# First queries and keys in halves of partitions, constants made by GpSimd, 28 constant products at the start, first values scaled in two parts

## The chip, the cores and the metric

The kernel runs on one core of one Trainium2 chip. The metric is the device time of one execution in microseconds (us), median of several runs. Four compute engines share the work: TensorE (matrix products; PE in the tables, PEld its weight loads), VectorE (DVE), ScalarE (ACT) and GpSimd (POOL). SyncE (SP) issues most loads and stores; ScalarE's queue issues some.

## The reference, cut to what matters

Retention attention over 8 batches and 8 heads of 576 positions with 64 values each, in fp32, then a mixture of 8 experts over the 4608 resulting rows of 512 values.

```python
scores = scale * np.matmul(q, k.transpose(0, 1, 3, 2))
rel = pos[:, None] - pos[None, :]
Dmat = np.where(rel >= 0, gamma[:, None, None] ** rel[None, :, :], 0.0)
ret = scores * Dmat[None, :, :, :]
return np.matmul(ret, v).astype(np.float32)
...
x = np.ascontiguousarray(attn_out.transpose(0, 2, 1, 3)).reshape(B * S, H * D)
...
expert_idx = np.argmax(logits, axis=1)
gate_w = probs[np.arange(N), expert_idx]
for e in range(E):
    mask = expert_idx == e
    h = np.maximum(x[mask] @ w1[e], 0.0)
    out[mask] = gate_w[mask, None] * (h @ w2[e])
```

## The kernel before

The 4608 rows are taken as 36 tiles of 128 rows, all 8 heads at once; a batch is 4.5 tiles. The first 140 us or so are attention (18 stages of two tiles), with the routing to experts woven in; the rest are the experts one after the other, each product made of three with operands split in a high and a low part.

For tile t, `qkt[t]` holds queries and keys turned (partition = position inside a head; partitions 0 to 63 are one head of each pair and 64 to 127 the other; four pairs), `kvt[t]` keys and values by rows. `emit_A(t)` makes the scores of a tile: for each pair p and half h a product of 64 partitions, to the banks `pa`; then VectorE masks them with the triangle `tri` into `pm`. `turn_k(t)` turns the keys of the first four tiles on TensorE with the identity `ident` (in tile 0 in two halves, to `prow` and `pa[2]`), and ScalarE copies them to `kvt`. `scale_v(t, ...)` scales the values by a power of the decay on GpSimd. `emit_U(t)` adds keys times values to the state (bank `pst`), which ScalarE copies to `T`. `emit_O(t)` multiplies the masked scores with the values to `po`. `decay(k)` makes the factors `gsb` on GpSimd.

The order of the instructions on each engine is that of the code (the schedule is manual); semaphores between engines are set from what each instruction reads and writes. `load_qk` and `load_kv` issue on SyncE; six tiles can be held, and a load of a later tile waits until TensorE has done with the buffer. Tile 0 alone is loaded from two queues: one half of `qkt[0]` by SyncE, followed by the table `cs`, and the other by ScalarE, followed by the values of tile 0.

Before the first scores, TensorE multiplies a constant matrix of bf16 ones with itself `NWARM` times, into `prow` and with no use of the result. In this time VectorE clears some tiles and, as soon as `cs` has landed, makes `tri` and `ident` by comparing the column number `iota` with the partition number `part`, both from `cs`.

Of the kernel before, what the change touches and what calls it, by code (L numbers as in the profile page):

```python
# [15 lines left out]
ALU = mybir.AluOpType  # L16
AX = mybir.AxisListType

P = 128
B, H, S, D = 8, 8, 576, 64  # L20
NP = H // 2
# [17 lines left out]
RW = 1032  # L39
XO = 520  # L40
BIG = 1.0e6
NWARM = 40
NO = NT + 2
HD = P // 2
QD = P // 4
# [6 lines left out]
KT = 9  # L52
# [49 lines left out]
def retention_moe(ctx: ExitStack, tc: tile.TileContext, qk, kv, embT, tau, w1, w2, cst, out):  # L102
    nc = tc.nc
# [26 lines left out]
    def mm(*args, **kw):  # L130
        pe[:] = [nc.tensor.matmul(*args, **kw)]  # L131
        return pe[0]
# [10 lines left out]
    def cc(name):  # L143
        o, w = _C[name]
        return cs[:, o : o + w]
# [24 lines left out]
    ident = keep.tile([P, P], F32, name="ident")  # L170
# [383 lines left out]
    with ExitStack() as att:  # L554
# [11 lines left out]
        qkt, kvt = {}, {}  # L566
# [13 lines left out]
        taub = ap.tile([P, 1], F32, name="taub")  # L580
        qkt[0] = qkp.tile([P, NP, 2, P], F32, name="qkt")
        kvt[0] = qkp.tile([P, 2, H, D], F32, name="kvt")
        nc.sync.dma_start(out=qkt[0][:, : NP // 2], in_=qk[0][:, : NP // 2])
        nc.scalar.dma_start(out=qkt[0][:, NP // 2 :], in_=qk[0][:, NP // 2 :])
        nc.sync.dma_start(out=cs, in_=cst[:, :_FIRST])
        nc.scalar.dma_start(out=kvt[0][:, 1], in_=kv[0][:, 1])
        load_qk(1)
# [14 lines left out]
        warm = psm.tile([P, 512], F32, name="m")  # L602
        for _ in range(NWARM):
            mm(warm[:, :P], one, one, start=True, stop=True)

        tri = ap.tile([P, P], F32, name="tri")
        trix = ap.tile([P, P], F32, name="trix")
        onef = ap.tile([P, P], F32, name="onef")
        iota, part = cc("iota"), cc("part")
        vx = ap.tile([P, H, D], F32, name="vx")  # L610
        E32 = ap.tile([P, NP, EW], F32, name="E32")
        nc.vector.memset(ones, 1.0)
        nc.vector.memset(onef, 1.0)
        nc.vector.memset(half, 0.5)
        nc.vector.memset(tok_all[:, 3 * NT :], 0.0)
        nc.vector.memset(ovs[:, 0:1], 0.0)
        nc.vector.memset(E32, 0.0)
        nc.gpsimd.memset(vx[:D], 0.0)
        nc.vector.tensor_scalar(out=tri, in0=iota, scalar1=part, scalar2=None, op0=ALU.is_ge)
        nc.vector.tensor_scalar(out=ident, in0=iota, scalar1=part, scalar2=None, op0=ALU.is_equal)  # L620

        def constants():
            nc.vector.tensor_copy(trix, tri)
# [25 lines left out]
        def embeddings_scale():  # L649
# [3 lines left out]
            nc.vector.tensor_tensor(  # L653
                out=E32[:, :, :NE], in0=emb, in1=en.unsqueeze(1).broadcast_to([P, NP, NE]), op=ALU.mult
            )
# [5 lines left out]
        gneg = cc("gneg").rearrange("p (t h) -> p t h", t=KT)  # L661
# [12 lines left out]
        def scale_v(t, eng):  # L674
            if t >= NT:
                return
            v = kvt[t][:, 1]
            eng.tensor_tensor(  # L678
                out=v, in0=v, in1=gneg[:, t % KT].unsqueeze(2).broadcast_to([P, H, D]), op=ALU.mult
            )  # L680
            if t % KT == 4:
                eng.tensor_copy(vx[D:], v[D:])

# [111 lines left out]
        def xpair(x, p):  # L795
            return x[..., p & 1, (p >> 1) * P : (p // 2 + 1) * P]
# [21 lines left out]
        def route_logits(b):  # L818
# [4 lines left out]
            for p in range(NP):  # L823
                for g in range(GT):
                    mm(
                        ps[g * EW : (g + 1) * EW, :P],
                        E32[:, p, :],
                        xpair(x[:, g], p),
# [38 lines left out]
        for b in range(NG):  # L867
            s0 = 2 * b + 2
            if s0 < HS:
                at((s0, 1.5), lambda b=b: (on(pa[2]), route_logits(b)))  # L870
                if s0 < LATE:
                    at((s0, 1.8), lambda b=b: (on(pa[2]), route_turn(b, False)))
                    at((s0, 3), lambda b=b: (keep_logits(b), route_head(b)))
                else:
                    at((s0, 3), lambda b=b: (on(pa[2]), route_turn(b), route_head(b)))
                if s0 + 1 < LATE:
                    at((s0 + 1, 1.7), lambda b=b: (on(pa[1]), rank_sum(b)))
                    at((s0 + 1, 2), lambda b=b: rank_slot(b))
                else:
                    at((s0 + 1, 2), lambda b=b: (on(pa[1]), route_rank(b)))  # L880
            if s0 + 2 < HS:
                if s0 + 2 < LATE:
                    at((s0 + 2, 1), lambda b=b: route_onehot(b))
                    at((s0 + 2, 1.7), lambda b=b: (on(pa[1]), route_table(b, False)))
                    at((s0 + 2, 2), lambda b=b: table_add(b))
                else:
                    at((s0 + 2, 3), lambda b=b: route_onehot(b))
                    at((s0 + 3, 2), lambda b=b: (on(pa[2]), route_table(b)))
            if b == EARLY - 1:
                at((s0 + 3, 1.7), lambda: (on(pa[0]), route_bump()))  # L890
                at((s0 + 2, 3), lambda: slots_to_tokens(0, 3))
                at((s0 + 2, 3), lambda t=2 * s0 + 8: scale_v(t, nc.gpsimd))
                for i in range(3):
                    at((s0 + 2, 3), lambda i=i: gather(0, i, EARLY * GT * P))
# [17 lines left out]
        emit_A(0)  # L912
        turn_k(0)
        scale_v(0, nc.gpsimd)
        scale_v(1, nc.gpsimd)
        decay(0)
        decay(1)
# [4 lines left out]
        for s in range(HS):  # L922
            t, u = 2 * s, 2 * s + 1
# [74 lines left out]
    with ExitStack() as moe:  # L998
# [3 lines left out]
        hs = mw.tile([P, 2, NF, CAP], F32R, name="hs")  # L1002
# [403 lines left out]
        for e in range(1, NE):  # L1406
            n = e + 1
# [61 lines left out]
            o = (bank[4], bank[5], bank[6], bank[4], bank[7])  # L1469
# [122 lines left out]
    with tc.If(ntile > 0):  # L1592
        with ExitStack() as ov:
            op = ov.enter_context(tc.tile_pool(name="op", bufs=1))
# [8 lines left out]
                out=io8, in0=cc("iota")[:, :NE], scalar1=float(ES), scalar2=None, op0=ALU.mult  # L1603
# [4 lines left out]
                out=sel, in0=eidx_all.unsqueeze(2).broadcast_to([P, NT, NE]), in1=io8, op=ALU.is_equal  # L1608
            )
            nc.vector.tensor_tensor(  # L1610
                out=sel, in0=sel, in1=ovs[:, :NE].unsqueeze(1).broadcast_to([P, NT, NE]), op=ALU.mult
# [12 lines left out]
                out=tok, in0=entry[:, :, 0], scalar1=float(P), scalar2=cc("part"), op0=ALU.mult, op1=ALU.add  # L1624
            )
            nc.vector.tensor_scalar(out=tok, in0=tok, scalar1=float(1 - P), scalar2=None, op0=ALU.add)
            for t in range(NT):
                nc.gpsimd.indirect_dma_start(
                    out=od[:, :],
                    out_offset=bass.IndirectOffsetOnAxis(ap=dsti[:, t : t + 1], axis=0),  # L1630
                    in_=tok[:, t : t + 1],
# [8 lines left out]
                out=te,  # L1640
                in0=cc("iota")[:, :NO].unsqueeze(2).broadcast_to([P, NO, NE]),
                in1=ovs[:, 1:].unsqueeze(1).broadcast_to([P, NO, NE]),
                op=ALU.is_ge,
# [7 lines left out]
            with tc.For_i(0, ntile, 1) as i:  # L1651
# [9 lines left out]
                    out=of[:, 0:1], in0=ent[:, 0:1], scalar1=-1.0, scalar2=0.0, op0=ALU.add, op1=ALU.max  # L1661
                )
                nc.vector.tensor_scalar(
                    out=of[:, 2:3], in0=ent[:, 0:1], scalar1=0.0, scalar2=BIG, op0=ALU.is_equal, op1=ALU.mult
# [6 lines left out]
                    out=go,  # L1671
                    out_offset=None,
                    in_=gd[:, :],
# [4 lines left out]
                    out=xo,  # L1678
                    out_offset=None,
                    in_=xd[:, :],  # L1680
# [29 lines left out]
                for f in range(NF):  # L1710
# [4 lines left out]
                    out=out[:, :],  # L1715
                    out_offset=bass.IndirectOffsetOnAxis(ap=oi[:, 1:2], axis=0),
                    in_=yo,
# [47 lines left out]
```

## Time and profile before

| | us |
|---|---|
| median of 3 runs | 552.0 (551.15, 552.0, 554.64) |
| profiled execution | 551.2 |
| its span, first to last instruction | 549.3 |
| TensorE busy in the span | 542.1 |
| TensorE's weight loads | 490.9 |
| VectorE | 406.9 |
| ScalarE | 359.0 |
| GpSimd | 213.2 |

The profiled execution is one run; times in its rows are counted from the start of the span. The profiled run's own time is 1.9 us longer than its span.

### The profile page before, as it was taken

How to read it: one execution, taken by the hardware profiler on the slowest of the kernel's cores; microseconds unless marked ns; L12 is line 12 of the kernel's file. 1: busy time of each engine (PE TensorE's matmuls, PEld its weight loads, DVE VectorE, ACT ScalarE, POOL GpSimd, SP SyncE). 2: the span in 40 equal slices, each digit the busy share in tenths (PEclk: the TensorE clock that was granted, in tenths of full speed). 3: DMA queues.
4: the chain of work that ended last, by engine and by line, in shares of the span. 5: the costliest groups of instructions: out<-in, count | busy, mean ns of one | idle time of the engine just before them, and what ended most of it. 6: DMA issues, size and time to landing. Idle time of an engine off the chain costs nothing. (4 is left out here: it accounts for less than half of the span.)

```text
span 549.3 us, 13219 instructions
## 1 busy us (share of the span) xinstructions
PE 542.1 (99%) x5119; PEld 490.9 (89%) x5119; DVE 406.9 (74%) x892; ACT 359.0 (65%) x656; POOL 213.2 (39%) x192
## 2 busy tenths in 40 slices
PE   9999999999999999999999999999999999999996
PEld 8999998889898889889988988998998899889984
DVE  3777789887786877995896899589689848957400
ACT  2455567665846786785786778578777857857311
POOL 4863222337446155067028415702840660161021
PEclk9999999999999999999999999999999999999999
DMA  8999999999567749457836945783692578351001
GB/s 316 384 338 363 392 398 388 371 380 257 193 129 217 195 133 283 76 151 219 185 79 190 277 80 133 228 188 97 178 277 67 152 243 162 94 176 51 4 38 50
DMA packets 83221, 111.70 MB, mean 203 GB/s; under 512 B 48151, under 2 KB 48443, under 8 KB 83136
## 3 DMA queue, kind: packets, MB, share of 16 engines
q1 hardware_dynamic: 75120, 90.00, 55.2%
q0 software_dynamic: 7680, 19.95, 11.0%
q8 instruction: 61, 1.00, 0.7%
q10 hardware_dynamic: 336, 0.54, 0.3%
q14 instruction: 24, 0.20, 0.1%
HBM read 81.10 MB, written 19.94 MB: 184 GB/s over the span
## 5 line engine op out<-in xcount | busy, mean ns | idle before, releaser
L1186 POOL DMA_INDIRECT out<-y,sid x40 | 51.6, 1290 | 157.4 <-ACT y L1182 137.8
L131 PE MATMUL pst<-w2f,hs 128*128 128x512 f32 x360 | 86.6, 390 | 0.0
L131 PE MATMUL po<-w2f,hs 128*128 128x512 f32 x371 | 86.5, 389 | 0.0
L131 PEld LDWEIGHTS po<-w2f,hs 128*128 128x128 f32 x371 | 69.4, 188 | 14.3
L131 PEld LDWEIGHTS pst<-w2f,hs 128*128 128x128 f32 x360 | 66.9, 188 | 13.2
L198 DVE TENSOR_TENSOR w2f<-wraw,w2f 128x1024 fp32r<-128x1024 f32 x32 | 39.1, 1223 | 42.0 <-ACT w2f L194 41.9
L678 POOL TENSOR_TENSOR kvt<-kvt,cs 128x512 f32<-128x512 f32 x36 | 38.3, 1069 | 66.1 <-DMA kvt<-kv 59.0
L442 ACT COPY graw<-graw 128x1024 uint16<-128x1024 uint16 x37 | 50.4, 1363 | 11.5 <-DMA graw<-graw 11.5
L421 POOL DMA_INDIRECT gt<-gd,gid x40 | 46.9, 1173 | 18.4 <-issue 11.6
L131 PE MATMUL prow<-w2f,hs 128*128 128x512 f32 x192 | 46.0, 390 | 0.0
L131 PE MATMUL pa<-xxf,w0f 128*128 128x304 f32 (+3 forms) x312 | 45.5, 297 | 0.0
L695 DVE TENSOR_TENSOR pm<-pa,tri 128x512 f32<-128x512 f32 x64 | 40.0, 682 | 6.9 <-PE pa L131 6.7
L131 PEld LDWEIGHTS pa<-xxf,w0f 128*128 128x128 f32 x312 | 43.0, 188 | 0.1
L131 PEld LDWEIGHTS prow<-w2f,hs 128*128 128x128 f32 x192 | 36.1, 188 | 7.5
L131 PE MATMUL pa<-xsf,w0f 128*128 128x384 f32 (+3 forms) x240 | 38.9, 312 | 0.0
L131 PE MATMUL pa<-qkt 64*128 64x128 f32 x576 | 38.7, 281 | 0.0
L482 DVE TENSOR_TENSOR graw<-graw 128x128 f32<-128x128 f32 x140 | 34.6, 289 | 5.2 <-ACT graw L442 4.0
L492 ACT CAST xxf<-graw 128x128 fp32r<-128x128 f32 x70 | 31.7, 458 | 10.3 <-DVE graw L482 9.9
L194 ACT CAST w2f<-wraw 128x1024 fp32r<-128x1024 f32 x32 | 33.6, 1051 | 6.5 <-DMA wraw<-w 6.4
L131 PEld LDWEIGHTS pa<-qkt 64*128 64x128 f32 x576 | 34.5, 189 | 3.6 <-issue 3.1
L131 PEld LDWEIGHTS pa<-xsf,w0f 128*128 128x128 f32 x240 | 36.2, 188 | 0.3 <-DVE hs L1074 0.3
L131 PE MATMUL po<-pm,kvt 128*64 128x128 f32 (+1 forms) x640 | 35.7, 263 | 0.1
(207 smaller groups left out, 1115.8 us busy)
## 6 DMA issues: line engine op xcount, KB each, us to landing
wraw<-w SPq DMA_DIRECT2D x64, 512.0 KB, 4.4
qkt<-qk SPq DMA_DIRECT2D x35, 512.0 KB, 6.8
kvt<-kv SPq DMA_DIRECT2D x32, 512.0 KB, 8.2
xd<-xw SPq DMA_DIRECT2D x36, 256.0 KB, 4.9
kvt<-kv SPq DMA_DIRECT2D x3, 256.0 KB, 6.6
gt<-gd,gid POOLq DMA_INDIRECT x40, 3.9
out<-y,sid POOLq DMA_INDIRECT x40, 4.0
graw<-xd,gid POOLq DMA_INDIRECT x26, 4.1
```

Of the source, the lines that this page charges most:

```text
L131: pe[:] = [nc.tensor.matmul(*args, **kw)]
L194: nc.scalar.copy(self.to[:, 0, c * 1024 : (c + 1) * 1024], self.raws[c])
L198: nc.vector.tensor_tensor(out=self.to[:, 1, c * 1024 : (c + 1) * 1024], in0=self.raws.pop(c), in1=hi.bitcast(F32), op=ALU.subtract,)
L421: nc.gpsimd.indirect_dma_start(out=g[:, i : i + 1], out_offset=None, in_=gd[:, :], in_offset=bass.IndirectOffsetOnAxis(ap=gid[:, a : a + 1 ...
L442: copy(t[:, :DM].bitcast(U16).rearrange("p (n h) -> p h n", h=2), t[:, XO : XO + DM].bitcast(U16).rearrange("p (h n) -> p h n", h=2),)
L482: nc.vector.tensor_tensor(out=v[:, 2 * k : 2 * k + 2], in0=a, in1=b, op=ALU.subtract)
L492: nc.scalar.copy(x[:, 0], u)
L678: eng.tensor_tensor(out=v, in0=v, in1=gneg[:, t % KT].unsqueeze(2).broadcast_to([P, H, D]), op=ALU.mult)
L695: nc.vector.tensor_tensor(out=pm[:, h], in0=banks[h].rearrange("p (c n) -> p c n", c=NP), in1=m.unsqueeze(1).broadcast_to([P, NP, P]), op= ...
L1186: sc = nc.gpsimd.indirect_dma_start(out=out[:, :], out_offset=bass.IndirectOffsetOnAxis(ap=sid[:, a : a + 1], axis=0), in_=ys[i], in_offse ...
```

## The change

It has four parts, all at the beginning of the program. The two halves of `qkt[0]` are cut by partitions (0 to 63 and 64 to 127, all four pairs each) and no longer by pairs. `ident` and `tri` are made by GpSimd from the matrix of ones `onef`, which VectorE clears first now, with no use of `cs`. `NWARM` is 28 in place of 40. The values of tile 0 are scaled in two products of four heads each; the other tiles as before.

```diff
-NWARM = 40
+NWARM = 28
...
-        nc.sync.dma_start(out=qkt[0][:, : NP // 2], in_=qk[0][:, : NP // 2])
-        nc.scalar.dma_start(out=qkt[0][:, NP // 2 :], in_=qk[0][:, NP // 2 :])
+        nc.sync.dma_start(out=qkt[0][:D], in_=qk[0][:D])
+        nc.scalar.dma_start(out=qkt[0][D:], in_=qk[0][D:])
...
+        nc.vector.memset(onef, 1.0)
+        for to, op in ((ident, ALU.is_equal), (tri, ALU.is_ge)):
+            nc.gpsimd.affine_select(
+                out=to, in_=onef, pattern=[[1, P]], compare_op=op, fill=0.0, base=0, channel_multiplier=-1
+            )
         nc.vector.memset(ones, 1.0)
-        nc.vector.memset(onef, 1.0)
...
         nc.gpsimd.memset(vx[:D], 0.0)
-        nc.vector.tensor_scalar(out=tri, in0=iota, scalar1=part, scalar2=None, op0=ALU.is_ge)
-        nc.vector.tensor_scalar(out=ident, in0=iota, scalar1=part, scalar2=None, op0=ALU.is_equal)
...
-            eng.tensor_tensor(
-                out=v, in0=v, in1=gneg[:, t % KT].unsqueeze(2).broadcast_to([P, H, D]), op=ALU.mult
-            )
+            n = H if t else H // 2
+            for o in range(0, H, n):
+                hs = slice(o, o + n)
+                eng.tensor_tensor(
+                    out=v[:, hs],
+                    in0=v[:, hs],
+                    in1=gneg[:, t % KT, hs].unsqueeze(2).broadcast_to([P, n, D]),
+                    op=ALU.mult,
+                )
```

On GpSimd, from the barrier at the program's start to the scaling of the values of tile 1 (`kvt_137` are the values of tile 0, `kvt_144` those of tile 1; ISA is a set-up instruction of the engine; a bracket names the engines and DMA queues that a row waits for), this stood before:

```order
L1761 UNCONDITIONAL_BRANCH [waits barrier_Pool_Activation_PE_DVE_SP_gather]
L618 MEMSET vx_208 64x512
L678 ISA
L678 TENSOR_TENSOR kvt_137<-kvt_137,cs_83 128x512 [waits DMAHW3_49,DMAHW2_49]
L678 TENSOR_TENSOR kvt_144<-kvt_144,cs_83 128x512 [waits DMAHW5_49]
```

And this stands there now:

```order
L1769 UNCONDITIONAL_BRANCH [waits barrier_Pool_Activation_PE_DVE_SP_gather]
L614 ISA
L614 AFFINE_SELECT ident_101<-onef_195 128x128 [waits DVE_49]
L614 AFFINE_SELECT tri_193<-onef_195 128x128
L622 MEMSET vx_196 64x512
L683 TENSOR_TENSOR kvt_137<-kvt_137,cs_83 128x256 [waits DMAHW3_49,DMAHW2_49]
L683 TENSOR_TENSOR kvt_137<-kvt_137,cs_83 128x256
L683 TENSOR_TENSOR kvt_144<-kvt_144,cs_83 128x512 [waits DMAHW5_49]
```

The two selections and the set-up instruction came in front of the clear of `vx`, and the one product of 512 columns became two of 256.

On TensorE, from the second half of the scores of tile 0 to its state product (`qkt_136` is tile 0; `pa0` and `pa1` are the banks of the two partition halves), before:

```order
L131 MATMUL pa0_73<-qkt_136 128x128 [waits DMAHW0_49]
L131 MATMUL pa1_74<-qkt_136 128x128
L131 MATMUL pa0_73<-qkt_136 128x128
L131 MATMUL pa1_74<-qkt_136 128x128
L135 MATMUL prow_78<-ident_101,qkt_136 128x128 [waits DVE_49]
L135 MATMUL prow_78<-ident_101,qkt_136 128x128
L135 MATMUL pa2_75<-ident_101,qkt_136 128x128 x2
L131 MATMUL pst_77<-kvt_137 64x64 [waits Activation_49,Pool_49]
L131 MATMUL pst_77<-kvt_137 64x64 x3
L131 MATMUL pst_77<-kvt_137 64x64 [waits Activation_49]
```

And now, from the end of the constant products:

```order
L131 MATMUL prow_78<-const-bfloat16-1.0 128x128
L131 MATMUL pa0_73<-qkt_136 128x128 [waits DMAHW1_49]
L131 MATMUL pa1_74<-qkt_136 128x128 [waits DMAHW0_49]
L131 MATMUL pa0_73<-qkt_136 128x128
L131 MATMUL pa1_74<-qkt_136 128x128
```

The wait for ScalarE's load (DMAHW0) moved from the fifth score product to the second. The turns behind them wait for GpSimd in place of VectorE, and the fifth state product waits for GpSimd too.

## Rows read from the trace of the kernel before

**Rows 1.** The page's first part: busy us, share of the span, instructions.

```profile
PE 542.1 (99%) x5119; PEld 490.9 (89%) x5119; DVE 406.9 (74%) x892; ACT 359.0 (65%) x656; POOL 213.2 (39%) x192
```

**Rows 2.** Waits of TensorE's weight loads: total us, times, longest us.

```profile
PEld pa L135 <- issue: 1.2, 3, 0.8
```

**Rows 3.** Timeline from 0 to 18 us: start, us, then idle time before it.

```profile
0.72 0.52 POOL L618 MEMSET vx<- 64x512 f32 x1 [0.29 <-POOLq L1756]
0.72 0.41 ACTq L584 DMA_DIRECT2D qkt<-qk  x1
...
0.73 4.18 PEld L131 LDWEIGHTS <-const-bfloat16-1.0 128*128 128x128 bf16 x40 [0.73 <-issue]
...
0.82 0.17 DVE L612 MEMSET ones<- 128x128 bf16 x1 [0.82 <-PEq L1756]
...
5.11 1.27 PEld L131 LDWEIGHTS pa<-qkt 64*128 64x128 f32 x16 [0.20 <-issue]
...
5.45 0.29 DVE L619 TENSOR_SCALAR tri<-cs 128x128 f32<-128x128 f32 x1 [4.10 <-DMA cs<-cst]
...
5.90 1.04 POOL L678 TENSOR_TENSOR kvt<-kvt,cs 128x512 f32<-128x512 f32 x1 [4.66 <-DMA kvt<-kv]
...
6.50 0.44 PE L135 MATMUL prow<-ident,qkt 128*128 128x128 f32 x2
6.61 1.29 DVE L695 TENSOR_TENSOR pm<-pa,tri 128x512 f32<-128x512 f32 x2 [0.68 <-PE pa L131]
...
6.98 0.37 ACT L716 COPY kvt<-prow 128x256 f32<-128x256 f32 x1 [4.04 <-PE prow L135]
...
7.46 0.58 PEld L131 LDWEIGHTS pst<-kvt 128*64 128x64 f32 x16 [0.54 <-POOL kvt L678]
...
7.92 0.89 PEld L131 LDWEIGHTS po<-pm,kvt 128*64 128x64 f32 x16
```

**Rows 4.** DMA: issues (us to landing) in 0.7:1.2, packets in 2:3, then 5:6.

```profile
qkt<-qk ACTq DMA_DIRECT2D x1, 256.0 KB, 3.8
qkt<-qk SPq DMA_DIRECT2D x1, 256.0 KB, 3.6
...
q1 hardware_dynamic: 73, 0.15, 44.1%
...
q1 hardware_dynamic: 89, 0.36, 91.0%
```

**Rows 5.** Stretch 4 to 5 us: five engines' busy us, granted clock, DMA share, GB/s.

```profile
4.00:5.00 1.00, 1.00 (x12) 0.91 (x9) 0.00 (x0) 0.00 (x0) 0.00 (x0) 1.00 1.02 318
```

**Rows 6.** TensorE's timeline in short stretches of tile 0's scores; first number: earliest start.

```profile
5.49 0.64 PE L131 MATMUL pa<-qkt 64*128 64x128 f32 x6
5.70 0.54 PE L131 MATMUL pa<-qkt 64*128 64x128 f32 x6
5.85 0.50 PE L131 MATMUL pa<-qkt 64*128 64x128 f32 x6
5.96 0.50 PE L131 MATMUL pa<-qkt 64*128 64x128 f32 x6
...
6.30 0.28 PE L131 MATMUL pa<-qkt 64*128 64x128 f32 x2
```

**Rows 7.** GpSimd by form, first 40 us; then DMA packets from 1.0 to 1.75 us.

```profile
L678 POOL TENSOR_TENSOR kvt<-kvt,cs 128x512 f32<-128x512 f32 x12 | 12.4, 1041 | 9.2 <-DMA kvt<-kv 9.1
L667 POOL TENSOR_TENSOR gsb<-csb 128x256 f32<-128x256 f32 x18 | 10.6, 617 | 0.7 <-DMA csb<-cst 0.7
...
DMA packets 0, 0.00 MB, mean 0 GB/s; under 512 B 0, under 2 KB 0, under 8 KB 0
```

**Rows 8.** Load of tile 5 (SyncE, then DMA view of its issue) and scores of tiles 4 and 5.

```profile
7.97 0.33 SPq L570 DMA_DIRECT2D qkt<-qk  x1
...
qkt<-qk SPq DMA_DIRECT2D x1, 512.0 KB, 8.0
...
16.72 2.06 PE L131 MATMUL pa<-qkt 64*128 64x128 f32 x32
```

## The prediction

> **What bounds the kernel now.** I read first the busy shares, then the waits of TensorE's weight loads, then the first 18 us instruction by instruction. The shares show TensorE at work for 542.1 of 549.3 us [rows 1]. Its weight loads show why nothing but TensorE's own row of work matters: over the whole span no single wait of theirs behind the start is longer than the 0.8 of [rows 2]. So a tenth of a microsecond that TensorE's row starts sooner is a tenth off the end, unless something fixed in time (a load) catches it later. All four edits lie in the first 9 us. The question is when the scores of tile 0 can start, and what then holds TensorE.
>
> The reader is to see this in the first stretch [rows 3]: 40 constant products hold TensorE until their last weights are in at 0.73 + 4.18 = 4.91; 0.20 later, at 5.11, the scores of tile 0 start. Their operands had landed: the two column halves, the slower issued at 0.72 [rows 3], took 3.8 and 3.6 us [rows 4], so 4.52 at the latest. It is the constant products that are waited for. Behind the scores stand the turns of the keys (6.50), their copies on ScalarE (6.98), the state product pst (7.46) and the output product po (7.92), which also waits for VectorE's masking (6.61 + 1.29 = 7.90).
>
> **TensorE's clock in that stretch.** The 40 weight loads of the constant products take 4.18 us, 0.105 each [rows 3], and each product has 128 columns: that is the 1.2 GHz level, though the column of the granted clock says 1.00 there [rows 5]. The scores start at the slow step too: 0.21 from 5.49 to 5.70 for a pair of products, and 0.11 from 5.85 to 5.96 [rows 6]. So the 2.4 GHz level came between 5.70 and 5.85. This sets the worth of an earlier start: work that is moved ahead of 5.85 costs twice as much.
>
> **Twelve constant products fewer.** They end 12 x 0.105 = 1.26 us sooner, with the last weights at 3.65; TensorE then waits for data instead. The start becomes the later half's landing and a hand-over that no row shows alone. It is no more than the 0.20 which TensorE lost between its last constant weights and the scores with the data long there [rows 3], and no less than nothing; I take 0.1.
>
> **Queries and keys by halves of partitions.** The bytes, the queues and the issue times stay; each half has 64 rows of 4 KB in place of 128 of 2 KB. Each pair of score products now needs both halves, where the first four products needed SyncE's half alone; with 3.6 and 3.8 us the halves differ by 0.2, so that costs nothing against a start at 5.11. What the trace says of the row size: 73 packets of 2 KB took 44.1% of 16 us between 2 and 3 us, 97 ns each, and 89 packets of mostly 4 KB took 91.0% between 5 and 6, 164 ns each [rows 4], so 4 KB costs 164 in place of 194. For the 256 packets of both halves on 16 engines that is 256 x 15 / 16 = 0.24 us less: landing at 4.3. From above, no row shows a load into 64 partitions; if it used half of the engines, the 256 x 97 / 16 = 1.55 us of transfer would be 3.1, and the landing 6.1. I take 4.3 to 4.52.
>
> The Trainium skill, page "DMA: Bandwidth & Descriptors", section "Rules for kernel authors", speaks against this edit: two transfers to disjoint partition halves run over the same 16 engines, so one should not bother. The trace agrees as far as it can, since the two column halves end 0.2 apart; by that rule the landing stays at 4.52, and the first of the two sums below holds.
>
> With a landing at 4.52 the eight pairs start at 4.62, 5.00 (the first step is 0.38, 5.11 to 5.49), 5.21, 5.42, 5.63, and then with the rise in between 5.83, 5.94, 6.05. The last start was 6.30 [rows 6]: gain 0.25. With a landing at 4.3 they start at 4.40, 4.78, 4.99, 5.20, 5.41, 5.62, 5.80, 5.91: gain 0.39. So of the 0.5 to 0.7 us at the start about half is paid back, since five or six pairs run at the lower level in place of three. I take **0.3**.
>
> **Does what follows keep it?** Turns at 6.2, copy at 6.7, first pst at 7.16, po at 7.62: each follows from TensorE or from an engine that TensorE releases, so each moves by 0.3. Masking too: it starts when the first bank is done (6.61 becomes 6.3).
>
> **Constants on GpSimd.** VectorE loses two operations of about 0.29 us each (tri at 5.45); it sat idle for 0.68 after them [rows 3], so nothing on the path. GpSimd gains two selections of 128x128. It is idle from 1.24 until 5.90 [rows 3, 7]. Their cost isn't in the trace. From below, a quarter of the 0.52 that a clear of 512 columns takes, 0.13; from above, the 0.617 of a two-input product of 256 columns. I take 0.4 each, nearer to the latter: waiting for onef (cleared first on VectorE, 0.82 + 0.17), ident is there by 1.5 and tri by 1.9, the clear of vx by 2.4. Needed at 6.2. The cover is 3.5 us of idle GpSimd; it is gone only if the set-up instruction ahead of them is slow (below).
>
> **First values in two parts.** GpSimd starts at 5.90, when the values land. Two products of 128x256 at 0.617 give the first half at 6.52 and the second at 7.13, against one at 6.94 now [rows 3, 7]. The first pst is wanted at 7.16 and its second half some 0.25 later: neither form is waited for, so the edit is worth nothing up to a gain of 0.5 elsewhere. GpSimd ends 0.19 later and covers that with its idle time: ahead of the first 12 scalings it waits 9.1 us in all for values to land [rows 7].
>
> **What could catch it.** The DMA engines are full once the loads run (a share of 1.02 from 4 to 5 us [rows 5]), so loads don't come sooner. The tightest load behind tile 0 is that of queries and keys of tile 5: issued at 7.97, landed 8.0 later at 15.97, used in the second half of the 2.06 us of scores from 16.72, at about 17.6 [rows 8]. Margin 1.6: the gain passes. Later loads are issued when TensorE frees a buffer, and move with it.
>
> **Sum.** The profiled execution took 551.2 (span 549.3 and 1.9 around it); less 0.3 it is 550.9. The median of the three runs shown is 552.0; of these with the profiled one (551.15, 551.2, 552.0, 554.64) the middle is 551.6. I forecast from that: 551.6 - 0.3 = **551.3**. A change of under 1% (5.5 us) can't be told from none here, and nothing in this change is that large.
>
> **Rivals.**
> *The higher clock comes later* (the slower side). TensorE now idles from 3.7 to about 4.5, between the constant products and the scores, where it idled for 0.20 [rows 3]. If this delays the rise from 5.8 to after tile 0, twice the time goes to three pairs of scores (+0.3), four turns at 0.11 (+0.4), pst (0.58, +0.5) and po (0.89, +0.9) [rows 3, 6]: up to +2.1, of which the waits for the copy and the mask hide part, at a guess 0.5; less the 0.3, net about +1.3, **552.9**. It decides from any delay of over 0.3 us. Against it: the gap is small against the 5 us of work ahead of the rise. 0.12.
>
> *GpSimd is late.* Ahead of its first real operation stands a set-up instruction (ISA), which moves in front of the selections. Now GpSimd idles 4.66 us between it and the first scaling; the profile gives this to the landing of the values, and no DMA packet moves from 1.0 to 1.75 [rows 3, 7]. But were it all set-up, the selections would start at 5.4, ident would come at 5.8, tri at 6.2, vx at 6.7, the halves of the values at 7.3 and 8.0, where pst's second half stands at 7.7 now: +0.3, **551.9**. 0.10.
> The Trainium skill, page "GPSIMD Engine Reference", section "2. Architecture", says that the first call of a freshly loaded kernel pays about 6 us with no visible instruction. The trace shows at most 4.7; by 6 us, an estimate from that page, the second half of the values would come at 9.3 and the time would be 553.2.
>
> *The start is swallowed*: the halves land later than now, or a load catches TensorE. Against it the margin of 1.6 us. **551.6**, 0.15.
>
> *More than forecast*: landing at 4.1 gives starts from 4.2 and a gain of 0.45; and the one "issue" pause of 0.8 us [rows 2], of which no engine is the cause, may move as 24 instructions fewer stand ahead of it. Down to **550.5**, 0.13.
>
> **How the numbers follow.** 0.50 for the forecast, 551.3. The rivals span 550.5 to 552.9; three runs of one kernel lay 3.5 us apart, so I add some at both ends: 549.9 to 553.4. Faster by over 1% would need 5.5 us: 0.01. Slower by over 1%: 0.02. Within: 0.97.
>
> **What would show it.** In the profile after: 28 constant products ending near 3.8; scores from 4.4 to 4.7 with a pause before them; the step halving between 5.6 and 6; two selections on GpSimd before 3 us; turns at 6.2, po at 7.6; the scores of tile 4 at 16.4 in place of 16.72. It is wrong if the slow step lasts beyond tile 0, if the selections start after 5, or if the scores still start after 5.

## The result, and the profile after

The changed kernel takes 555.85 us (median of 11 runs, 553.33 to 558.88) against 551.72 for the kernel before (11 runs): a ratio of 1.0071, 95% interval 1.0043 to 1.0098. That is 3.9 us (the medians lie 4.1 apart), within 1% as forecast, but slower, and above the top of the range. The profiled execution took 555.85 with a span of 554.0, 4.7 more than before.

First the busy shares of the changed kernel, then its longest waits of the weight loads for data (total us, times, longest us):

```profile
PE 543.9 (98%) x5107; PEld 491.9 (89%) x5107; DVE 407.5 (74%) x890; ACT 359.4 (65%) x656; POOL 215.1 (39%) x195
```

```profile
PEld pa L131 <- DMA qkt<-qk: 2.2, 2, 1.2
```

TensorE does the same work as in [rows 1] and still holds the time. New is the second line: two waits for queries and keys, 2.2 us in all, in a place where [rows 2, 3] had none over 0.8. The timeline from 0 to 26 us shows where (start, us, then idle time before it):

```profile
0.79 0.58 SPq L583 DMA_DIRECT2D qkt<-qk  x1
...
0.80 2.90 PEld L131 LDWEIGHTS <-const-bfloat16-1.0 128*128 128x128 bf16 x28 [0.80 <-issue]
...
0.89 0.17 DVE L612 MEMSET onef<- 128x128 f32 x1 [0.89 <-PEq L1764]
...
1.13 0.29 POOL L614 TENSOR_SCALAR_AFFINE_SELECT ident<-onef 128x128 f32<-128x128 f32 x1 [0.63 <-DVE onef L612]
...
4.94 0.50 PEld L131 LDWEIGHTS pa<-qkt 64*128 64x128 f32 x2 [1.24 <-DMA qkt<-qk]
...
6.36 1.78 PEld L131 LDWEIGHTS pa<-qkt 64*128 64x128 f32 x14 [0.92 <-DMA qkt<-qk]
...
8.37 0.29 PEld L135 LDWEIGHTS prow<-ident,qkt 128*128 128x128 f32 x2 [0.22 <-POOL kvt L683]
...
9.54 1.00 PEld L131 LDWEIGHTS pst<-kvt 128*64 128x64 f32 x16 [0.45 <-issue]
...
10.39 1.51 PEld L131 LDWEIGHTS po<-pm,kvt 128*64 128x64 f32 x16
...
12.07 0.97 PEld L131 LDWEIGHTS pa<-qkt 64*128 64x128 f32 x16 [0.17 <-issue]
```

The constant products end at 0.80 + 2.90 = 3.70 (3.65 forecast). The first scores then wait until 4.94, and after two loads TensorE waits again, until 6.36. Behind that all is slow: pst takes 1.00 where [rows 3] have 0.58, and po 1.51 in place of 0.89. Only from 12.07 on is the work at its old pace: the scores of tile 1, 16 loads in 0.97.

This last row is the yardstick for everything below, since it stands behind all that the four edits touch. In the timeline of the kernel before it reads:

```profile
8.98 0.97 PEld L131 LDWEIGHTS pa<-qkt 64*128 64x128 f32 x16 [0.17 <-issue]
```

So TensorE's row is 12.07 - 8.98 = 3.09 late when tile 0 is done. The scores of tile 4 start at 19.81 against 16.72 [rows 8], 3.09 late as well: nothing is paid back. The remaining 1.6 of the span's 4.7 comes later and in pieces; runs of one kernel lie 5 us apart, and such pieces are treated with run e3 and in the last section.

Where the 2.2 us of waiting come from, the DMA view of the first two issues shows (last number: us to landing):

```profile
qkt<-qk SPq DMA_DIRECT2D x1, 256.0 KB, 4.1
qkt<-qk ACTq DMA_DIRECT2D x1, 256.0 KB, 5.5
```

Against 3.6 and 3.8 of [rows 4]: landed at 4.9 and 6.3 in place of 4.33 and 4.52. The same view of the stretch from 2 to 3 us says how, first of the kernel before and then of the changed one:

```profile
DMA packets 135, 0.28 MB, mean 276 GB/s; under 512 B 0, under 2 KB 0, under 8 KB 135
...
q1 hardware_dynamic: 73, 0.15, 44.1%
q10 hardware_dynamic: 62, 0.13, 35.9%
```

```profile
DMA packets 31, 0.13 MB, mean 127 GB/s; under 512 B 0, under 2 KB 0, under 8 KB 31
...
q1 hardware_dynamic: 31, 0.13, 91.7%
```

Before, the packets of both queues ran side by side. Now only SyncE's queue runs, and its 31 packets of 4 KB fill 91.7% of 16 engines for 1 us: 0.917 x 16 / 31 = 473 ns each, where [rows 4] gave 164 for 4 KB. The engines read as busy, and carry half as much. These 473 ns hold for this stretch alone; runs e1 and e7 below show that they are no fixed price of the 64 partitions. From 4 to 5 us (five engines' busy us, granted clock, DMA share, GB/s):

```profile
4.00:5.00 1.00, 0.06 (x1) 0.06 (x1) 0.00 (x0) 0.00 (x0) 0.00 (x0) 1.00 1.04 204
```

204 GB/s at a full share, against 318 in [rows 5].

The trace's record of single packets parts the delay of the later half, 1.8 us, in three. The first packet moves at 2.16 in place of 1.77; the loads are issued 0.06 to 0.08 later, and an issue takes 0.58 where [rows 3] have 0.41. SyncE's packets then run from 2.16 to 4.01 and ScalarE's from 3.28 to 5.17, where before they ran from 1.77 to 4.05 and from 1.98 to 4.14: 3.01 for both halves in place of 2.37. And the landing comes 1.15 behind the end of the last packet, in place of 0.40. That is 0.39, 0.64 and 0.75; the slower packets are a good third of it.

### The profile page after: what moved, and what is told of

Its sections match the earlier page's. It is cut to its first block, busy times and chain, and to the rows that moved or that the text cites. A ratio compares the mean times of both kernels' runs of the same rounds, so it can differ in the third digit from the quotient of the medians.

```text
span 554.0 us, 13198 instructions
## 1 busy us (share of the span) xinstructions
PE 543.9 (98%) x5107; PEld 491.9 (89%) x5107; DVE 407.5 (74%) x890; ACT 359.4 (65%) x656; POOL 215.1 (39%) x195
## 5 line engine op out<-in xcount | busy, mean ns | idle before, releaser
L683 POOL TENSOR_TENSOR kvt<-kvt,cs 128x512 f32<-128x512 f32 (+1 forms) x37 | 38.8, 1053 | 66.0 <-DMA kvt<-kv 64.8
L131 PE MATMUL pa<-qkt 64*128 64x128 f32 x576 | 40.2, 284 | 1.9 <-DMA qkt<-qk 1.6
```

Source lines behind the costliest of these rows:

```text
L683: eng.tensor_tensor(out=v[:, hs], in0=v[:, hs], in1=gneg[:, t % KT, hs].unsqueeze(2).broadcast_to([P, n, D]), op=ALU.mult,)
```

## The experiments

My theory after the result (A): the halves of partitions land one after the other, and late; the rest of the 3.1 is TensorE's lower clock, kept by its idling. The rivals: 28 products alone put the clock's rise off (B); GpSimd's selections or their place slow the loads (C). "Rise" in the expectations is the point at which the trace's record of the granted clock goes to its upper level for the first time: 11.7 us in the changed kernel, 5.8 before. Ahead of that point the column of the granted clock reads 1.00 as well and tells nothing; in the rows the rise shows as the pace of the scores: 16 loads in 0.97 at the upper level.

| run | products | queries and keys of tile 0 | constants, values | ratio to the kernel before, interval | rise of the clock | tile 1's scores start |
|---|---|---|---|---|---|---|
| before | 40 | column halves | as before | 1 | 5.8 | 8.98 |
| after | 28 | partition halves | changed | 1.0071, 1.0043 to 1.0098 | 11.7 | 12.07 |
| e1 | 40 | partition halves | as before | 1.0040, 1.0011 to 1.0070 | 5.3 | 10.42 |
| e2 | 28 | column halves | as before | 1.0014, 0.9982 to 1.0045 | 3.4 | 8.41 |
| e3 | 28 | column halves | changed | 1.0017, 0.9983 to 1.0051 | 5.1 | 8.37 |
| e4 | 64 | partition halves | changed | 1.0035, 1.0006 to 1.0065 | 3.6 | 9.92 |
| e5 | 40 | partition halves | changed | 1.0035, 1.0009 to 1.0062 | 4.9 | 10.01 |
| e6 | 40 | partition halves in two parts each | changed | 1.0014, 0.9984 to 1.0044 | 3.5 (down again at 10.3) | 12.19 |
| e7 | 40 | one load of 128 rows | changed | 1.0031, 0.9999 to 1.0064 | 6.8 | 9.75 |
| e8 | 40 | column halves | changed | 1.0001, 0.9969 to 1.0032 | 6.0 | 9.16 |

The ratios are good to some 1.6 us, the last two columns are one execution of each, but the last is good to a hundredth; where both speak they are read together.

**e1, the partition halves alone.**

```diff
-        nc.sync.dma_start(out=qkt[0][:, : NP // 2], in_=qk[0][:, : NP // 2])
-        nc.scalar.dma_start(out=qkt[0][:, NP // 2 :], in_=qk[0][:, NP // 2 :])
+        nc.sync.dma_start(out=qkt[0][:D], in_=qk[0][:D])
+        nc.scalar.dma_start(out=qkt[0][D:], in_=qk[0][D:])
```

> The kernel before with nothing but the two loads of tile 0 cut by partitions; 40 constant products stay. Theory A (the cut makes the later half land late, and TensorE's idle time behind it delays the 2.4 GHz level): the later half lands near 6.3 us in place of 4.5, ident and tri come after 6.5 since their table waits behind, scores end after 7; the time is 2 to 4 us above the kernel before. Theory B (the short run of constant products is what delays the clock, the late half costs only its own 1.2 us): with 40 products the step halves before 7 us and the time is about 1.2 above. Theory C (GpSimd's early work slows the loads): halves land by 4.7 and the time is within 0.5 of the kernel before.

The DMA view of the first issues, then the timeline:

```profile
qkt<-qk SPq DMA_DIRECT2D x1, 256.0 KB, 4.8
qkt<-qk ACTq DMA_DIRECT2D x1, 256.0 KB, 3.7
...
cs<-cst SPq DMA_DIRECT2D x1, 164.5 KB, 5.2
```

```profile
5.62 0.97 PEld L131 LDWEIGHTS pa<-qkt 64*128 64x128 f32 x16 [0.70 <-DMA qkt<-qk]
...
6.82 1.07 DVE L620 TENSOR_SCALAR ident<-cs 128x128 f32<-128x128 f32 x1
...
7.94 0.20 PEld L135 LDWEIGHTS prow<-ident,qkt 128*128 128x128 f32 x2 [1.35 <-DVE ident L620]
```

The second half is late with nothing else changed: 5.6 against 4.5. Here ScalarE's half came first, in the changed kernel SyncE's; one of the two always waits. The next loads of the two queues are late too, and as the constants are here made from cs (5.2 us to landing, 4.2 in the kernel before), ident holds the turns for 1.35. Why ident itself took 1.07 in place of 0.28 stays open. The first part of A, the late half, is shown, and C can't explain it, as GpSimd makes no constants here. Its second part is not: with 40 products the clock rose at 5.3, as B had it, and the scores ran at the upper level (0.97). The late half alone doesn't bring the late clock.

**e2, 28 products alone; e3, the change without the partition halves.** e2 sets only `NWARM = 28`; e3 is the changed kernel with the two loads of e1's diff as they were.

> The kernel before with 28 constant products in place of 40 and nothing else. Theory A: the halves land at 4.5, the scores start at 4.6 to 4.7, the step halves before 7 us, the time is 0 to 0.4 us below the kernel before. Theory B: the scores start at 4.65 as well, but the step halves only after 9 us, and the time is 1.5 to 2.5 above. Theory C: as A.

> The changed kernel with the loads of tile 0 cut by pairs as before; 28 products, constants by GpSimd and the values in two parts stay. Theory A: halves at 4.5, scores at 4.65, 0.2 to 0.5 us below the kernel before, about 4 below the changed kernel. Theory B: the clock comes after 9 us, 1.5 to 2.5 above the kernel before. Theory C: a half lands after 5.5 us although the cut is by pairs, 3 to 4 above.

The weight loads of e2:

```profile
0.73 2.83 PEld L131 LDWEIGHTS <-const-bfloat16-1.0 128*128 128x128 bf16 x28 [0.73 <-issue]
4.52 0.97 PEld L131 LDWEIGHTS pa<-qkt 64*128 64x128 f32 x16 [0.97 <-DMA qkt<-qk]
```

and of e3:

```profile
4.42 1.28 PEld L131 LDWEIGHTS pa<-qkt 64*128 64x128 f32 x16 [0.72 <-DMA qkt<-qk]
5.82 0.20 PEld L135 LDWEIGHTS prow<-ident,qkt 128*128 128x128 f32 x2
```

With column halves, 28 products do what I forecast and more: start at 4.4 to 4.5, and tile 1 reached 0.57 and 0.61 sooner than before. The clock is up by the scores in e2, and by the turns in e3 (0.20): B falls, since 28 products alone don't bring the late clock either. C falls too: with GpSimd's selections the halves landed at 4.6 at the latest.

The time shows no gain. In the profiles it is lost again at pauses for which no semaphore is waited, such as these in the attention stretch, e2 and then e3:

```profile
59.86 0.58 PEld L131 LDWEIGHTS pa<-xT,E 128*32 128x32 f32 x20 [0.94 <-issue]
```

```profile
60.13 0.58 PEld L131 LDWEIGHTS pa<-xT,E 128*32 128x32 f32 x20 [1.26 <-issue]
```

I took them at first for a consequence of the 28 products. The last section shows that kernels with 40 have such pauses too; whether 28 make them likelier stays open.

**e4, the changed kernel with 64 products.** Only `NWARM = 64`: TensorE works until 5.8, so that the clock is up whatever the halves do.

> The changed kernel with 64 constant products in place of 28: they last until about 6.7 us, past the landing of the later half. All theories: the step halves near 5.8 us, inside the constant products. Theory A: the scores run fast from 6.8 to 7.7 where the kernel before ended them at 6.58, so the time is 1.0 to 1.5 above the kernel before and 2.5 to 3 below the changed kernel: the clock was worth that much. If the clock was worth nothing, the time stays about 4 above.

The weight loads:

```profile
6.29 0.97 PEld L131 LDWEIGHTS pa<-qkt 64*128 64x128 f32 x16 [0.49 <-DMA qkt<-qk]
...
9.92 0.97 PEld L131 LDWEIGHTS pa<-qkt 64*128 64x128 f32 x16 [0.17 <-issue]
```

The second half is as late as in the changed kernel (5.4 us from issue, 6.25), but the scores run at the upper level, and tile 1 comes 0.94 behind that of before in place of 3.09. By the ratios e4 is 1.9 us slower than the kernel before, where A had 1.0 to 1.5.

**e5, the changed kernel with 40 products.**

> The changed kernel with 40 constant products in place of 28 (partition halves, selections on GpSimd and values in two parts stay). Theory A (the partition halves land one after the other, the second at 5.6 to 6.3, and TensorE's idling ahead of them, lengthened by the 12 products that are gone, put the clock's rise off to 11.7): the products end their weights near 4.9, the second half still lands at 5.6 to 6.3, the pause ahead of the scores shrinks to about 1, and the rise comes back to 5.1 to 6; the row behind po stands 0.9 to 1.5 behind that of before, against 3.1 in the changed kernel: 553 to 554.5. Rival (a late rise belongs to the late half alone, whatever runs ahead): rise after 9, row 2.5 to 3.5 behind, 555 to 556. On the pauses without a wait of 0.7 to 1.4 us at 59 to 64 and 98 to 101 us, which the three kernels with 28 products all show: if they hang on the place of an instruction in TensorE's row, the 24 instructions that are back move them, and the pauses stand at 90 to 92 as in the kernel before, or are under 0.5; if they are chance, they show at either place.

The weight loads:

```profile
0.80 4.15 PEld L131 LDWEIGHTS <-const-bfloat16-1.0 128*128 128x128 bf16 x40 [0.80 <-issue]
5.05 0.29 PEld L131 LDWEIGHTS pa<-qkt 64*128 64x128 f32 x2
6.40 0.96 PEld L131 LDWEIGHTS pa<-qkt 64*128 64x128 f32 x14 [1.05 <-DMA qkt<-qk]
7.49 0.20 PEld L135 LDWEIGHTS prow<-ident,qkt 128*128 128x128 f32 x2
8.41 0.66 PEld L131 LDWEIGHTS pst<-kvt 128*64 128x64 f32 x16 [0.50 <-POOL kvt L683]
8.95 0.89 PEld L131 LDWEIGHTS po<-pm,kvt 128*64 128x64 f32 x16
10.01 0.97 PEld L131 LDWEIGHTS pa<-qkt 64*128 64x128 f32 x16 [0.17 <-issue]
```

This run splits the loss, for this pair of profiles. Its 14 loads start at 6.40, those of the changed kernel at 6.36: the data are equally late. Twelve more products are the only difference, and tile 1 comes at 10.01 in place of 12.07. So 10.01 - 8.98 = 1.03 is lost without the lower clock (0.18 of it with column halves too, in e8; 0.85 to the late half), and the lower clock costs 2.06: from the 14 loads to the turns 2.01 against 1.09, from there to pst 1.17 against 0.92, to po 0.85 against 0.54, to tile 1 1.68 against 1.06, in sum 2.10 more, less the 0.04 of the earlier start. The two ratios differ by 2.0 us, though their intervals overlap. The 2.06 is no constant: e9 to e14 below give less in some executions.

**e6, quarters of 2 KB rows; e7, one load.** Both with 40 products. e6 asks whether the rows of 4 KB or the 64 partitions are slow:

```diff
-        nc.sync.dma_start(out=qkt[0][:D], in_=qk[0][:D])
-        nc.scalar.dma_start(out=qkt[0][D:], in_=qk[0][D:])
+        nc.sync.dma_start(out=qkt[0][:D, : NP // 2], in_=qk[0][:D, : NP // 2])
+        nc.scalar.dma_start(out=qkt[0][D:, : NP // 2], in_=qk[0][D:, : NP // 2])
+        nc.sync.dma_start(out=qkt[0][:D, NP // 2 :], in_=qk[0][:D, NP // 2 :])
+        nc.scalar.dma_start(out=qkt[0][D:, NP // 2 :], in_=qk[0][D:, NP // 2 :])
```

> The changed kernel with 40 constant products, and with each partition half of the first queries and keys loaded as two transfers of 64 rows of 2 KB (four transfers, the first pairs' quarter of each half first). If the late second half comes from the 4 KB rows, all four quarters land by 4.7 as the column halves of 2 KB rows did, the scores start near 5.1, and the time is 551.5 to 552.5. If it comes from loading into 64 partitions at a time, the last quarter still lands at 5.5 to 6.5; the scores of the first pairs start when the first quarters of both are there, by 4.9 to 5.5, and the rest wait: 552.5 to 554.5.

In e7 one line takes their place, `nc.sync.dma_start(out=qkt[0], in_=qk[0])`; the values on ScalarE's queue are then issued at once.

> The changed kernel with 40 constant products and the first queries and keys as one transfer of 128 rows of 4 KB on SyncE; ScalarE's first load is then that of the values. If 4 KB rows are what is slow, it lands at 5.5 or later. If the 64 partitions are, it lands by 4.5 to 4.9 (one queue has to issue all of it), and the scores start at 5.1 or just behind the landing: 551.5 to 552.5.

The bytes moved in the first 6.5 us tell it, in the DMA view of before, of the changed kernel, of e6 and of e7, in this order:

```profile
DMA packets 740, 1.53 MB, mean 235 GB/s; under 512 B 74, under 2 KB 202, under 8 KB 740
```

```profile
DMA packets 467, 1.05 MB, mean 162 GB/s; under 512 B 60, under 2 KB 188, under 8 KB 467
```

```profile
DMA packets 541, 0.88 MB, mean 136 GB/s; under 512 B 79, under 2 KB 202, under 8 KB 541
```

```profile
DMA packets 587, 1.50 MB, mean 231 GB/s; under 512 B 57, under 2 KB 185, under 8 KB 587
```

Rows of 4 KB over 128 partitions (e7) carry as much as the column halves; rows of 2 KB over 64 partitions (e6) carry even less than 4 KB ones. It is the 64 partitions: all ten profiles that load into 64 at a time moved 0.88 to 1.23 MB in that time, the six that load into 128 moved 1.42 to 1.53.

The landing of e7 alone would have said otherwise. It came at 5.5, which I had put down as the sign of slow 4 KB rows. But there the values' 256 KB run beside it: queries, keys, table and values of tile 0 are all in by 6.0, against 5.8 before and 7.1 in the changed kernel. So e7 is no gain all the same: the scores wait for all of the load and start at 5.56.

A single packet's time doesn't tell 64 partitions from 128. From 2 to 3 us, e1 (64) and e7 (128), both with rows of 4 KB on the queue shown:

```profile
q10 hardware_dynamic: 54, 0.22, 79.6%
```

```profile
q1 hardware_dynamic: 49, 0.20, 78.7%
```

That is 236 ns and 257 ns each, beside the 473 of the changed kernel.

In e6 the values came so late that pst waited for them, and the clock went down again. Its weight loads, then its stretches (granted clock third from the end):

```profile
9.47 0.31 PEld L131 LDWEIGHTS pst<-kvt 128*64 128x64 f32 x8 [2.57 <-POOL kvt L685]
...
10.28 1.59 PEld L131 LDWEIGHTS po<-pm,kvt 128*64 128x64 f32 x16
12.19 1.69 PEld L131 LDWEIGHTS pa<-qkt 64*128 64x128 f32 x16 [0.33 <-issue]
```

```profile
10.00:11.00 1.00, 0.95 (x16) 0.95 (x18) 0.00 (x0) 0.37 (x1) 1.00 (x1) 0.66 1.04 397
11.00:12.00 1.00, 1.00 (x12) 0.86 (x9) 0.00 (x0) 0.00 (x0) 0.52 (x1) 0.50 1.01 401
```

A pause of 2.57 us behind the turns; pst still runs at the upper level (8 loads in 0.31), and from 10.3 on the granted clock is 0.50, the 1.2 GHz level. The profiled execution was the longest of its ten (556.9; the median is 553.5), so this need not happen in each.

**e8, column halves and 40 products.** What is left of the change is the selections and the values in two parts.

> The changed kernel with column halves as before and 40 constant products: what is left of the change is the two selections on GpSimd and the values in two parts. My forecast priced these at nothing: landing 4.4 to 4.7, scores at 5.1, turns within 0.1 of 6.5, time within 0.5 of the kernel before. If the pauses without a wait near 60 and 98 us come from the number of instructions ahead of them, they are not there, as they are not in the kernel before. If they come from the selections or from the values in parts, they are there, and the time is 1 to 2 above.

Ratio 1.0001, tile 1 0.18 later. The weight loads:

```profile
5.18 1.32 PEld L131 LDWEIGHTS pa<-qkt 64*128 64x128 f32 x16 [0.20 <-issue]
...
7.54 0.66 PEld L131 LDWEIGHTS pst<-kvt 128*64 128x64 f32 x16 [0.50 <-POOL kvt L683]
```

0.07 of it is the start, 5.18 in place of 5.11 [rows 3], since the first constant product comes at 0.80 and not at 0.73 in every kernel with the selections; 0.08 is pst, 0.66 in place of 0.58, as in e3, e4, e5 and e7, the other kernels with the values in two parts. What its second eight wait for is not shown: their first load starts at 7.86, and the second part of the values was done at 7.13. The pauses near 60 and 98 us are not there (0.36 at most), which is what the expectation had for the count of instructions as their cause; but the kernel before, with the same count, has small ones there (last section).

**e9 to e14, the lower clock again.** e9 and e14 are the changed kernel unaltered; e10, e12 and e13 one kernel, the one before with partition halves and `NWARM = 28`; e11 is e3 with `NWARM = 14`. They ran on chips on which the kernel before took 560 to 579 us, with 11 to 18 us between its own runs, and no interval came out under 2% wide: e12 gave 1.0206 (1.0098 to 1.0315) and e13 1.0192 (1.0052 to 1.0333), the others no ratio. So the times that these expectations name are neither met nor missed, and only the first 13 us of the profiles are used.

> The changed kernel once more, unaltered, for a second profile. If the rise of TensorE's clock at 11.7 us belongs to this kernel (28 constant products and a second half that lands at 6.3), it comes again between 9 and 14, the row behind po of tile 0 stands about 3 us behind that of before, and the time is 554.5 to 557. If it was the chance of one execution, the rise comes by 7.5 us, the row stands 1 to 1.8 behind, and the time is 552.5 to 554.5. The second half lands at 5.6 to 6.4 either way.

> The kernel before with the partition halves and 28 constant products, constants still made on VectorE and the values in one part. Theory (the loss is the late second half plus a late rise of the clock when TensorE idles over 2 us ahead of the scores): all of the changed kernel's loss is here, 555 to 556.5 with a rise between 9 and 14 us; or 553.5 to 555 if the rise comes by 7.5 us in most executions. Rival (GpSimd's selections or the values in parts have a share): 1 to 2 us under the changed kernel, 553.5 to 554.5, with the rise late all the same.

> The changed kernel with column halves, which land by 4.7, and 14 constant products in place of 28, so that TensorE idles for about 2 us from 2.3 to 4.4 ahead of the scores, with no half that is late. If idling ahead of the scores is what puts the clock's rise off, it comes after 7.5 us and the scores, turns, pst and po of tile 0 run at the slow step: the row behind po at or behind that of the kernel before, where 28 products stood 0.7 ahead of it, time 553.5 to 556. If the late rise needs the late half, the rise comes at 3 to 6 us as with 28 products, the scores start at 4.4 to 4.5 and the row stands 0.5 to 0.9 ahead of that of before: 551 to 553.5.

> The kernel before with partition halves and 28 constant products once more, for its time: in the run before, all kernels of the call, the kernel before too, took some 20 us longer. The late second half and the late rise of the clock are both in its profile, and the row behind po stood 3.0 behind that of before, as in the changed kernel. Theory (these two are the whole loss, and GpSimd's selections and the values in parts cost nothing): 3 to 4.5 above the kernel before, as the changed kernel's 3.9. Rival (the rest of the change has a share): 1.5 to 2.5 above.

> The kernel before with partition halves and 28 constant products, beside the changed kernel. Theory (the late half and the late rise are the whole loss): within 1.5 of the changed kernel, and 3 to 4.5 above the kernel before. Rival (GpSimd's selections or the values in parts have a share): 1.5 to 2.5 above the kernel before, and the changed kernel above it by as much again.

> The changed kernel, unaltered, timed on the same chip as the one beside it. It came out 3.9 above the kernel before; its third profile should show the second half at 5.9 to 6.4, the rise at 11 to 13 and the row behind po 2.7 to 3.2 behind that of before. If the rise comes by 7.5 us in this one, the late rise is no fixed part of the loss.

The weight loads of e11, whose column halves landed at 4.8 and 5.0:

```profile
0.80 1.42 PEld L131 LDWEIGHTS <-const-bfloat16-1.0 128*128 128x128 bf16 x14 [0.80 <-issue]
4.83 1.78 PEld L131 LDWEIGHTS pa<-qkt 64*128 64x128 f32 x16 [2.62 <-DMA qkt<-qk]
...
8.86 1.38 PEld L131 LDWEIGHTS po<-pm,kvt 128*64 128x64 f32 x16
10.41 0.97 PEld L131 LDWEIGHTS pa<-qkt 64*128 64x128 f32 x16 [0.17 <-issue]
```

The scores wait 2.62 and then run slow, as does most of po: tile 1 comes 2.04 behind that of e3, 0.41 of it by the later start. So a long idling ahead of the scores keeps the clock down without any partition half. In the five new profiles with partition halves and 28 products (e9, e10, e12, e13, e14) tile 1 starts at 11.99, 12.22, 10.82, 11.01 and 11.24, each time with scores of 1.78 or 1.79 from about 6 and a rise at 11.9, 12.3, 9.7, 9.9 and 10.1: the late rise is no chance of one execution. It is there without the selections (e10, 12.22) as with them. How much it costs is chance: against the same kernel with 40 products the row is 1.98 and 1.23 later in e9 and e14 (e5: 10.01), and 1.80, 0.40 and 0.59 in e10, e12 and e13 (e1: 10.42). For e14 I had expected a rise at 11 to 13 and a row 2.7 to 3.2 behind that of before; it was 10.1 and 2.26. What the selections and the values in parts add to the time next to the late half, these runs could not tell; beside column halves e8 shows no difference in time (1.0001).

## Why the prediction was wrong

**The step that failed** is "Queries and keys by halves of partitions". I took a landing of 4.3 to 4.52, from the engines' 164 ns for 4 KB packets; those were loads over 128 partitions. With 64 the second half landed at 6.3, and at 5.6 to 6.4 in every kernel with such halves. "The issue times stay" was wrong (0.58 in place of 0.41), the packets of both halves took 3.01 us in place of 2.37, and the time from the last packet to the landing, for which I had no term, grew from 0.40 to 1.15. I had written down the right end, 6.1 "if it used half of the engines", as an upper bound that no row shows, and then priced it at nothing: in the rivals a late half is "The start is swallowed", 0.15, at 551.6. The engines did read as busy, so the mechanism of that bound isn't shown, only its size. Two of the signs of being wrong that I had named came: scores after 5, and the slow step through all of tile 0.

The Trainium skill, page "DMA: Bandwidth & Descriptors", section "Rules for kernel authors", advises against two transfers to disjoint partition halves, as they serialize, and for one transfer of 128 partitions. I read that as "no gain". The runs agree with the advice and make it a loss (one after the other in eight of the nine profiles with two halves; in e14 the packets of both ran together, and landed no sooner, at 6.0 and 6.2): 1.05 MB in the first 6.5 us with halves, 1.50 with one load (e7), 1.53 with column halves.

**The rival that joined it** is "The higher clock comes later". I gave it 0.12 and 552.9, and held against it that the gap was small, 0.8 us. With the late half it was 1.24 and 0.92 with two loads between. It cost 2.06 against e5, where I had 1.6 (2.1 less 0.5 hidden; net 1.3): 0.3 for three pairs of scores, where the whole set ran slow, 0.92, and 1.3 for the rest, where it was 1.18. The two rivals "swallowed" and "clock" were each priced alone: swallowed by 0, clock by a gap of 0.8. The late half brought on both, and together they make 3.09 in the profile: 551.6 + 3.1 = 554.7. The other 1.15 of the 555.85 lie behind tile 0 and stay open.

**Steps that held.** Twelve products fewer are worth what I said and somewhat more: loads end at 3.70 (3.65 forecast), and with column halves tile 1 is reached 0.57 to 0.61 sooner (e2, e3; 0.3 forecast), as the clock rose sooner there (3.4 and 5.1) than I had assumed (5.8). The selections took 0.29 each (0.4 forecast) and were done at 1.68 (1.9). So the rival "GpSimd is late" is out. The Trainium skill, page "GPSIMD Engine Reference", section "2. Architecture", says that the first call of a freshly loaded kernel pays about 6 us. No such time shows here: the first selection started at 1.13, at most 0.1 behind the end of its operand; whether it was such a call, no run shows. The values in two parts cost 0.08 (e8; nothing forecast). And GpSimd's constants do gain something where loads are late: without them ident held the turns in e1, and tile 1 comes at 10.42 against 10.01 with them (e5), though e1's second half landed 0.8 sooner.

**"The gain passes"** is neither shown nor refuted. e2 and e3 keep their 0.6 until 59 us, and then meet pauses of 0.9 to 1.3 that a run may or may not have (below). A gain of 0.3 to 0.6 can't be seen in a time that differs by 5 us from run to run. No version here beats the kernel before.

## What to carry to other kernels

Split a load for two queues by columns, not by partitions: each half should cover all 128 partitions. Work that only keeps TensorE busy ahead of the first real products is worth keeping up to the landing of their data; what it saves in cutting it (0.6 here) is less than what the lower clock costs when the data turn out later (1.2 to 2.1 in three profiles of the changed kernel). And when one edit makes data later and another removes what covered the wait, price the two together.

## What the runs showed of the hardware

**The slow halves.** Loads into 64 partitions at a time moved 0.88 to 1.23 MB in the first 6.5 us, loads into 128 moved 1.42 to 1.53, at the same share of the engines (1.04 and 1.02 from 4 to 5 us in the changed kernel and in that of before). Why is not settled by any run here.

**The clock goes down within a kernel's work.** In e6 a pause of 2.57 us was followed by a granted clock of 0.66, 0.50, 0.50 and 0.64 in the four microseconds from 10 to 14.

**Pauses on a row of 127 products.** I counted TensorE's products from the first constant one, in the profiles of before, after and e1 to e8. Between 10 and 135 us there are sixteen steps of some 0.4 us or more (0.40 to 1.37) from one weight load to the next without a semaphore to wait for, besides one at the lower clock in e6. They stand behind product 1111 (five), 1238, 1365, 1746 (two), 1872 or 1873 (six) and 2508, that is 1111 and 1, 2, 5, 6 and 11 times 127 more. They hold to the count, not to the place in the program: products more or fewer at the start only change which one is hit. Before has them at 1111 (0.50), 1746 (the "issue" pause of [rows 2]) and 1873; e2, e3 and the changed kernel at 1111 and 1872 or 1873; e4, e5 and e8 none. So 28 products are not needed for them. But at 1111 all nine profiles with 28 or 14 products have one, of 0.65 to 1.66, e9 to e14 among them, and of the seven with 40 or 64 only before and e1 (in e5, e6 and e7 the trace names VectorE for a wait there): whether fewer products make that one likelier stays open. On the chips of e9 to e14 there are also some twenty such steps off this row, from 127 to 133 us. A product is a weight load and a multiplication, so 127 are 254 instructions. The profile page of the changed kernel lists the queue that brings instructions:

```profile
q8 instruction: 61, 1.00, 0.7%
```

1.00 MB in 61 packets is 16 KB each. That TensorE waits there for its next block of instructions while loads fill the DMA engines fits both, but is argued, not shown; no run took the loads away, and it doesn't explain the steps off the row.
